# Weight loads move from SyncE's queue to ScalarE's, into ten raw slots and then five

## The chip, the cores and the metric

The kernel runs on one core of one Trainium2 chip. The metric is the time of one execution on the device in microseconds (us), lower is better. Five engines work side by side, each through its own instructions in the order in which they were placed: TensorE (PE, with its weight loads shown as PEld), VectorE (DVE), ScalarE (ACT), GpSimd (POOL) and SyncE (SP), which in this kernel issues every transfer (DMA). The transfers themselves run on 16 DMA engines.

## The reference

Causal attention with a decay, then a gated two-layer block, over 8 batches x 8 heads x 576 tokens x 64 (4608 tokens of 512 features, 2048 hidden):

```python
scores = scale * np.matmul(q, k.transpose(0, 1, 3, 2))
cum = np.cumsum(np.log(np.clip(f, 0.0001, 1.0)), axis=-1)
decay = cum[:, :, :, None] - cum[:, :, None, :]
scores = np.where(causal, -1000000000.0, scores + decay)
attn = np.exp(scores - np.max(scores, axis=-1, keepdims=True))
attn = attn / (np.sum(attn, axis=-1, keepdims=True) + 1e-09)
x = np.matmul(attn, v).transpose(0, 2, 1, 3).reshape(B * S, H * D)
h = x @ w_in
g = h * np.clip(h + 3.0, 0.0, 6.0) / 6.0
out = g @ w_out
```

`w_in` (512 x 2048) and `w_out` (2048 x 512) come as 64-bit floats, 8 MB each; everything else is 32-bit.

## The kernel before

The attention is walked over a list `VH` of stages. Batch 0 is cut in two so that the second layer block can start early: four stages "A" (two heads each, the first 256 queries) and eight stages "B" (one head each, the other 320 queries). Batches 1 to 7 are 56 stages "F" (one head each). For a stage of batch 0 the work is: `load_x` and `load_c` bring q, k and the decay rows; `parts` and `rests` split q and k in two (the low halves are copied between partitions by transfers `T<-TQ`, `T<-TK`); `natural` makes the scores once for the row maximum (PE tile `pn`, DVE `junk`, L490); `max_rows` turns the maxima (`mr`) and sends them by a small transfer `TQ<-mr` into the operand of the real scores; `scores` makes these on PE (`ps`, L548 to L551) and ACT takes the exponential (`pf`, L567; `pf_0` is that of the first stage); `av` multiplies with v (L702), and `x_move` transposes the result into `xT`. The decay rows for all stages come from `decay`: ACT takes a logarithm (`lf`, L169), DVE scans it (`cs`, L172 to L174), and four small transfers `TK<-cs` (L427) bring it to the first two stages.

The weights are brought in 16 chunks of `w_in` and 16 of `w_out`, each 128 x 1024 32-bit words (0.524 MB: 512 values of 64 bits on each of 128 partitions). `w_load` issues a chunk's transfer into a raw slot; `w_decode` makes a 32-bit float of it (ACT Prelu L250, two DVE instructions L251 and L252, which still read the slot) and then takes the sum of squares (ACT Square L256, which writes its junk into the slot, so a slot is free once its Square is done). After four chunks of `w_in` the scale of that group is found (`pow2_scale`), and each chunk is split into two 16-bit halves (`w_split`: ACT L283, and either PE `low` L286, L287 with ACT L288, or DVE L294). `w_out` has one scale for all 16 chunks, so its splits start only when its last chunk is decoded.

Raw slots: three tiles `ring`, which the F stages use for other things later, and for `w_in` three more in the later home of `w2`. Chunk k goes to slot k mod 6 (`w_in`) or k mod 3 (`w_out`). For `w_in` four or five chunks are asked for ahead (`W_AHEAD`). The first eight loads are `pinned`: they stand behind the latest small transfer of the attention in SP's queue.

The generators `w_in_work` and `w_out_work` are advanced by `w_step`, eight times in an A stage, five times in a B stage; `fill` advances the work of the second block (`h_unit`, L781 to L796; `out_unit`, L803 to L815). What is written this way is only a priority: a scheduler places every engine's instructions by a timeline that it works out itself, and gives them the semaphores. For the transfers of both queues it has eight completion counters, DMAHW0 to DMAHW7, which they take in turn; a transfer that takes a counter again waits until the one that had it before has landed.

Of the kernel before, what the change touches and what calls it, by code (L numbers as in the profile page):

```python
# [13 lines left out]
I32 = mybir.dt.int32  # L14
# [6 lines left out]
def kernel(  # L21
# [10 lines left out]
    nc = tc.nc  # L32
# [50 lines left out]
    W_RATE = (8, 5, 4)  # L83
    H_COST = 1.05
    F_RATE = (0.6, 0.45, 1.02)
    PIN = 0
    PIN0 = 1
    LOW_W = 0
    W_GAP = 5
# [11 lines left out]
    NSP = 3  # L101
    PL_POOL = ((3, ), ())
    NAT = ((1, 4, 0), (2, 3))
    B0_POOL = ((0, 0), (1, 1))
    W_AHEAD = (4, 5)
    W_ORDER = 0
    POOL_REST = ((0, 0, 0, 0), (0, 0, 0, 0))
    PIN_V = 1
# [22 lines left out]
    vst = cpool.tile([P, NCH, VR], F32, name="vst")  # L131
# [4 lines left out]
    xT = [cpool.tile([P, NCC, 2, TT // P, 2, 64], F16, name=f"xT{i}") for i in range(3)]  # L136
# [69 lines left out]
    def pinned():  # L206
        return tc.issue_after(small[-1]) if small else nullcontext()


    wide = w_in.dtype == mybir.dt.int64  # L210
    NW = 16
    CW = NCC * DFF // NW
    wsum = cpool.tile([P, 2 * NW], F32, name="wsum")
    ring = [cpool.tile([P, 2 * CW], I32, name=f"ring{i}") for i in range(NRING)]
    gTf = gT.bitcast(F32).rearrange("p a c t -> p (a c t)")
    w2f = w2.bitcast(F32).rearrange("p k a e -> p (k a e)")
    spare = w2.bitcast(I32).rearrange("p k a e -> p (k a e)")
    slots_out = [t[:, :] for t in ring]
    slots_in = slots_out + [spare[:, (2 * h + 9) * CW:(2 * h + 11) * CW] for h in range(NSP)]

    def w_chunk(i, k):

        if i == 0:
            j, c = divmod(k, NCC)
            cols = slice(j * CW, (j + 1) * CW)
            o = (2 * j + c % 2 + NW // 2 * (c // 2)) * CW
            return w_in[c * P:(c + 1) * P, cols], gTf[:, o:o + CW], [t[:, c, cols] for t in w1]
        return (
            w_out[k * P:(k + 1) * P, :], w2f[:, (k + 1) * CW:(k + 2) * CW],
            [w2[:, k, h, :] for h in range(2)],  # L230
        )

    def w_load(i, k, slots):
        src, x, _ = w_chunk(i, k)
        with pinned() if PIN or i == 0 and k < 8 else nullcontext():
            if wide:
                nc.sync.dma_start(slots[k % len(slots)], src.bitcast(I32))
            else:
                nc.sync.dma_start(x, src)

    def w_decode(i, k, slots):

        slot = slots[k % len(slots)]
        f32 = w_chunk(i, k)[1]
        if wide:
            i32 = f32.bitcast(I32)
            hf = slot.bitcast(F32).rearrange("p (n t) -> p n t", t=2)[:, :, 1]
            lo = slot.rearrange("p (n t) -> p n t", t=2)[:, :, 0]

            nc.scalar.activation(f32, hf, AF.Prelu, scale=2.0 ** -112, alpha=2.0 ** 32)  # L250
            nc.vector.tensor_scalar(i32, i32, 3, None, op0=ALU.logical_shift_left)  # L251
            nc.vector.scalar_tensor_tensor(  # L252
                i32, lo, 29, i32, op0=ALU.logical_shift_right, op1=ALU.bitwise_or
            )
        if i == 1 or not GRAM[k // NCC]:
            nc.scalar.activation(  # L256
                slot.bitcast(F32)[:, :CW], f32, AF.Square,
                accum_out=wsum[:, NW * i + k:NW * i + k + 1],
            )

    def w_gram(ks):

        pg = ps_m.tile([P, TT], F32, tag="mm", name=f"gram_{ks[0]}")[:, 0:P]
        n = len(ks) * CW // P
        for c in range(n):
            x = w_chunk(0, ks[c * P // CW])[1].bitcast(BF16)
            x = x.rearrange("p (n t) -> p n t", t=2)[:, c * P % CW:c * P % CW + P, 1]
            nc.tensor.matmul(pg, x, x, start=(c == 0), stop=(c == n - 1))
        junk = p2.tile([P, S], BF16, tag="junk", name=f"jg_{ks[0]}", bufs=1)
        nc.vector.tensor_tensor_reduce(  # L270
            junk[:, 0:P], pg, identf, 1.0, 0.0, ALU.mult, ALU.add,
            accum_out=wsum[:, ks[0]:ks[0] + 1],
        )
        return wsum[:, ks[0]:ks[0] + 1]
# [19 lines left out]
            nc.vector.scalar_tensor_tensor(lo, x, sc, hi, op0=ALU.mult, op1=ALU.subtract)  # L294

    def w_in_work():
        first, ahead = W_AHEAD
        for k in range(first):
            w_load(0, k, slots_in)
        yield  # L300
        for k in range(first, ahead):
            w_load(0, k, slots_in)
        for j in range(NG):
            ks = range(j * NCC, (j + 1) * NCC)
            for k in ks:
                if k + ahead < NW:
                    w_load(0, k + ahead, slots_in)
                w_decode(0, k, slots_in)
                yield
            pm = w_gram(ks) if GRAM[j] else w_sum(ks[0], ks[-1] + 1)  # L310
            yield
            yield from pow2_scale(pm, S1 + j, I1 + j, f"w0{j}")
            eye = None
            if PE_LOW[j]:
                eye = p2.tile([P, DM], F32, tag="o", name=f"eye{j}")[:, 0:P]
                nc.vector.tensor_scalar(
                    eye, identf, scol(S1 + j), -1.0, op0=ALU.mult, op1=ALU.mult
                )
            for k in ks:
                w_split(0, k, scol(S1 + j), eye)  # L320
                yield
            w_in_done.append(j)
# [591 lines left out]
    for i, (kind, n) in enumerate(VH):  # L914
        b, h = divmod(n, H)
# [4 lines left out]
        ahead = i + 2 < NV  # L920
# [99 lines left out]
```

## Time and profile before

| what | us |
|---|---|
| three runs without the profiler | 1083.75, 1084.57, 1087.27 |
| median | 1084.57 |
| the profiled execution | 1083.28 |
| its span, first to last instruction | 1081.5 |
| around the span | 1.8 |
| PE busy in it | 1010.1 |
| DVE, ACT, POOL busy in it | 719.7, 610.1, 413.1 |

The page of the profile gives the busy time of each engine and the span cut in 40 equal slices (27 us each). In the first slices lies what this change touches: the transfers of the weights, their decoding, stages A and B. A matmul's busy time is longer than the time after which the next one starts, so a PE that is shown busy throughout may still have room. An entry such as "idle before <-DMA ring" says what ended the idle time ahead of an instruction.

### The profile page before, as it was taken

How to read it: one execution, taken by the hardware profiler on the slowest of the kernel's cores; microseconds unless marked ns; L12 is line 12 of the kernel's file. 1: busy time of each engine (PE TensorE's matmuls, PEld its weight loads, DVE VectorE, ACT ScalarE, POOL GpSimd, SP SyncE). 2: the span in 40 equal slices, each digit the busy share in tenths (PEclk: the TensorE clock that was granted, in tenths of full speed). 3: DMA queues.
4: the chain of work that ended last, by engine and by line, in shares of the span. 5: the costliest groups of instructions: out<-in, count | busy, mean ns of one | idle time of the engine just before them, and what ended most of it. 6: DMA issues, size and time to landing. Idle time of an engine off the chain costs nothing.

```text
span 1081.5 us, 20281 instructions
## 1 busy us (share of the span) xinstructions
PE 1010.1 (93%) x7074; PEld 577.4 (53%) x7074; DVE 719.7 (67%) x1887; ACT 610.1 (56%) x1285; POOL 413.1 (38%) x505
## 2 busy tenths in 40 slices
PE   2799977988999999999999989999999999999998
PEld 2567854755555555555555545555555555444443
DVE  7869899876885688468865795689668841510520
ACT  4778656845764577356754674477447841621520
POOL 7344455335434445444544444454445420000000
PEclk9989989999999999999999999999999999999999
DMA  8866547767756666667576856675666651000001
GB/s 258 277 172 194 150 105 134 179 127 150 156 114 141 140 146 118 137 129 164 108 139 138 164 113 130 146 166 114 128 140 128 106 112 46 1 10 30 1 1 39
DMA packets 261650, 133.74 MB, mean 124 GB/s; under 512 B 229444, under 2 KB 231036, under 8 KB 261548
## 3 DMA queue, kind: packets, MB, share of 16 engines
q1 hardware_dynamic: 261548, 132.45, 54.7%
q8 instruction: 56, 0.92, 0.3%
q14 instruction: 46, 0.38, 0.1%
HBM read 47.93 MB, written 9.73 MB: 53 GB/s over the span
## 4 chain that ended last, share of the span: by engine, by line
PE 64%; DVE 12%; DMA 9%; issue 5%; ACT 5%; SPq 2%; POOL 2%; DVEq 0%; POOLq 0%; ACTq 0%
PE po L803 10%; PE po L804 10%; PE po L805 10%; PE ph L781 7%; PE ph L782 7%; PE ph L783 7%; DMA vst<-in_vS_dram 3%; PE pn L611 3%; PE pn L608 2%; DVE pp L619 2%; DVE ring L648 2%; DMA T<-TK 1%; DVE gT L796 1%; DMA w<-in_w_in_dram 1%; DVE r L794 1%
## 5 line engine op out<-in xcount | busy, mean ns | idle before, releaser
L781 PE MATMUL ph<-xT,w 128*128 128x512 f16 (+1 forms) x640 | 231.2, 363 | 14.5 <-DVE r L794 9.1
L782 PE MATMUL ph<-xT,w 128*128 128x512 f16 (+1 forms) x640 | 230.2, 363 | 0.0
L783 PE MATMUL ph<-xT,w 128*128 128x512 f16 (+1 forms) x640 | 230.0, 363 | 0.0
L631 ACT ACTIVATE pp<-pp,nb 128x192 f32<-128x192 f32 x280 | 138.5, 552 | 148.8 <-DVE nb L625 145.8
L804 PE MATMUL po<-w,gT 128*128 128x512 f16 x576 | 216.3, 381 | 6.1 <-DVE w L294 6.1
L805 PE MATMUL po<-w,gT 128*128 128x512 f16 x576 | 215.9, 381 | 0.0
L803 PE MATMUL po<-w,gT 128*128 128x512 f16 x576 | 213.6, 381 | 1.1 <-ACT o L814 0.8
L648 DVE TENSOR_TENSOR ring<-pp,ring 128x128 f16<-128x128 f32 (+2 forms) x216 | 131.5, 622 | 84.1 <-ACT ring L645 83.2
L791 ACT ACTIVATE r<-ph,bias_r,SC 128x256 f32<-128x256 f32 (+7 forms) x272 | 144.4, 570 | 28.6 <-PE ph L783 27.9
L794 DVE SCALAR_TENSOR_TENSOR r<-r,ph 128x512 f32<-128x512 f32 (+1 forms) x160 | 100.1, 627 | 88.9 <-ACT r L791 88.6
L458 POOL TENSOR_TENSOR T<-ST,T 64x576 fp32r<-64x576 f32 (+1 forms) x68 | 101.2, 1488 | 143.2 <-DMA T<-TK 133.4
L619 DVE CUSTOM_DVE_ANT_0 pp<-pn,W 128x192 f32<-128x192 f32 x280 | 122.9, 482 | 20.6 <-PE pn L611 16.6
L796 DVE TENSOR_TENSOR gT<-r,gT 128x512 f16<-128x512 f32 (+1 forms) x160 | 118.3, 743 | 27.4 <-ACT gT L795 26.6
L795 ACT CAST gT<-r 128x512 f16<-128x512 f32 (+1 forms) x160 | 91.8, 575 | 75.9 <-DVE r L794 75.8
L608 PE MATMUL pn<-TK,TQ 68*128 68x192 f32 x336 | 124.1, 383 | 5.8 <-issue 5.0
L611 PE MATMUL pn<-T,T 128*128 128x192 f32 x336 | 113.5, 368 | 4.3 <-POOL T L458 4.3
L645 ACT CAST ring<-pp 128x192 f16<-128x192 f32 x280 | 112.9, 452 | 0.0
L455 POOL TENSOR_TENSOR T<-ST,TQ 64x576 fp32r<-64x576 f32 (+2 forms) x68 | 97.6, 1435 | 24.8 <-PE pn L611 18.2
L654 POOL TENSOR_TENSOR ring<-pp,ring 128x128 f16<-128x128 f32 x96 | 61.5, 641 | 105.5 <-ACT ring L645 83.7
L782 PEld LDWEIGHTS <-w 128*128 128x128 f16 x640 | 62.7, 99 | 65.8 <-issue 20.9
L805 PEld LDWEIGHTS <-gT 128*128 128x128 f16 x576 | 56.8, 99 | 74.9 <-issue 13.7
L781 PEld LDWEIGHTS <-w 128*128 128x128 f16 x640 | 63.1, 99 | 62.2 <-issue 14.3
(136 smaller groups left out, 1703.4 us busy)
## 6 DMA issues: line engine op xcount, KB each, us to landing
ST<-in_qk_dram SPq DMA_DIRECT2D x64, 288.0 KB
T<-TK SPq DMA_DIRECT2D x64, 144.0 KB
out_dram<-o SPq DMA_DIRECT2D x36, 256.0 KB
ring<-in_w_out_dram SPq DMA_DIRECT2D x16, 512.0 KB
T<-TQ SPq DMA_DIRECT2D x56, 144.0 KB
vst<-in_vS_dram SPq DMA_DIRECT2D x7, 1040.0 KB
ring<-in_w_in_dram SPq DMA_DIRECT2D x9, 512.0 KB
w<-in_w_in_dram SPq DMA_DIRECT2D x7, 512.0 KB
```

Of the source, the lines that this page charges most:

```text
L608: nc.tensor.matmul(dst, TQ[i][0:D + 4, qs], TK[i][0:D + 4, a:e], start=True, stop=False)
L611: nc.tensor.matmul(dst, T7[j][:, qs], T1[j][:, a:e], start=False, stop=True)
L619: nc.vector.tensor_tensor_reduce(pp[:r, w:w + kw], pn[:r, o:o + kw], W[:r, 4 * P + r - kw:4 * P + r], 1.0, -3.0e38, ALU.add, ALU.max, accu ...
L631: nc.scalar.activation(x_, x_, AF.Exp, bias=nb[:r, e0 + x:e0 + x + 1], scale=0.125)
L648: eng.tensor_tensor(hl[:r, a:a + c * P], pp[:r, at[c] + 64:at[c] + kw], hl[:r, h0[c] + 64:h0[c] + kw], op=ALU.subtract,)
L781: nc.tensor.matmul(ph, w1[0][:, cc, fs_], xh, start=(cc == 0), stop=False)
L782: nc.tensor.matmul(ph, w1[0][:, cc, fs_], xl, start=False, stop=False)
L783: nc.tensor.matmul(ph, w1[1][:, cc, fs_], xh, start=False, stop=(cc == NCC - 1))
L791: nc.scalar.activation(r[:, a:e], ph[:, a:e], AF.Relu, bias=bias_r, scale=scol(A1 + NG * b + fc * NG // NFC))
L803: nc.tensor.matmul(po, gT[:, 0, fc, ts_], w2[:, fc, 0, :], start=(fc == 0), stop=False)
L804: nc.tensor.matmul(po, gT[:, 0, fc, ts_], w2[:, fc, 1, :], start=False, stop=False)
L805: nc.tensor.matmul(po, gT[:, 1, fc, ts_], w2[:, fc, 0, :], start=False, stop=(fc == NFC - 1))
```

## The change

All 32 loads of weights are issued from ACT's queue instead of SP's. `w_in` gets ten raw slots: the three `ring` tiles, two in `vst` (where v of batch 1 and later will stand), two in `xT[1]` (a tile of transposed attention output, first written in stage B), and the three in `w2`. All ten loads are asked for at once, and each further load directly behind the decoding that frees its slot. `w_out` gets five: the `ring` tiles and the two in `vst`. The pinning and its constants are gone.

```diff
-    slots_out = [t[:, :] for t in ring]
-    slots_in = slots_out + [spare[:, (2 * h + 9) * CW:(2 * h + 11) * CW] for h in range(NSP)]
+    vsp = vst.bitcast(I32).rearrange("p c e -> p (c e)")
+    xsp = xT[1].bitcast(I32).rearrange("p a h c l t -> p (a h c l t)")
+    slots_out = [t[:, :] for t in ring] + [vsp[:, 2 * h * CW:2 * (h + 1) * CW] for h in range(2)]
+    slots_in = slots_out + [xsp[:, 2 * h * CW:2 * (h + 1) * CW] for h in range(2)]
+    slots_in += [spare[:, (2 * h + 9) * CW:(2 * h + 11) * CW] for h in range(NSP)]
...
     def w_load(i, k, slots):
         src, x, _ = w_chunk(i, k)
-        with pinned() if PIN or i == 0 and k < 8 else nullcontext():
-            if wide:
-                nc.sync.dma_start(slots[k % len(slots)], src.bitcast(I32))
-            else:
-                nc.sync.dma_start(x, src)
+        if wide:
+            nc.scalar.dma_start(slots[k % len(slots)], src.bitcast(I32))
+        else:
+            nc.scalar.dma_start(x, src)
...
     def w_in_work():
-        first, ahead = W_AHEAD
-        for k in range(first):
+        ahead = len(slots_in)
+        for k in range(ahead):
             w_load(0, k, slots_in)
         yield
-        for k in range(first, ahead):
-            w_load(0, k, slots_in)
         for j in range(NG):
             ks = range(j * NCC, (j + 1) * NCC)
             for k in ks:
+                w_decode(0, k, slots_in)
                 if k + ahead < NW:
                     w_load(0, k + ahead, slots_in)
-                w_decode(0, k, slots_in)
                 yield
```

Line numbers of the changed kernel differ by one or two (the load is L237 before and L238 after; `pf` is L567 and L566). What the scheduler makes of it shows at three places.

**The start of ACT.** Before, ACT's first rows lead straight to the logarithm `lf`, and its first Prelu reads the first chunk:

```order
L161 ACT_TABLE_LOAD
L161 ACTIVATE warm<-warm 1x1 [waits DVE_49]
L169 ACTIVATE lf<-fs 64x576 [waits DVE_49]
L170 ACT_TABLE_LOAD
L170 ACTIVATE warm<-lf 1x1 [waits Activation_49]
L250 ACTIVATE gT<-ring_123 128x512 [waits DMAHW2_49]
```

In the changed kernel (`ring`, `vst`, `xT`, `w` are the slots):

```order
L238 DMA ring_123<-in_w_in_dram 128x1024
L159 ACT_TABLE_LOAD
L159 ACTIVATE warm<-warm 1x1 [waits DVE_49]
L238 DMA ring_124<-in_w_in_dram 128x1024
L238 DMA ring_125<-in_w_in_dram 128x1024
L238 DMA vst<-in_w_in_dram 128x1024
L238 DMA vst<-in_w_in_dram 128x1024 [waits DMAHW0_49]
L238 DMA xT_118<-in_w_in_dram 128x1024 [waits DMAHW1_49]
L238 DMA xT_118<-in_w_in_dram 128x1024 [waits DMAHW2_49]
L238 DMA w_115<-in_w_in_dram 128x1024 [waits DMAHW3_49]
L238 DMA w_115<-in_w_in_dram 128x1024 [waits DMAHW4_49]
L238 DMA w_115<-in_w_in_dram 128x1024 [waits DMAHW5_49]
```

The logarithm comes right behind these rows: ten issues now stand ahead of it, and the last six each wait for a counter, that is for an earlier transfer to land (DMAHW0 was taken by the first chunk, DMAHW3 by the second, DMAHW5 by the third, the others by the loads of f and q, k).

**SP's queue, from the decay rows to the first row maxima.** Before (TK_96 is the operand of the first stage, TK_97 of the second):

```order
L427 DMA TK_96<-cs 2x1x256 [waits DMAHW1_49]
L427 DMA TK_97<-cs 2x1x256 [waits DMAHW2_49,Pool_49]
L427 DMA TK_97<-cs 2x1x256 [waits DMAHW3_49]
L453 DMA T_101<-TQ_93 64x512 [waits DMAHW4_49,Pool_49]
L454 DMA T_99<-TK_96 64x512 [waits DMAHW5_49]
L869 DMA decay_dram<-cs 64x1152 [waits DMAHW6_49]
L237 DMA ring_125<-in_w_in_dram 128x1024 [waits DMAHW7_49,Activation_49]
L237 DMA w_115<-in_w_in_dram 128x1024 [waits DMAHW0_49,Activation_49]
L454 DMA T_100<-TK_97 64x512 [waits DMAHW1_49,Pool_49]
L421 DMA TK_98<-decay_dram 2x2x256 [waits DMAHW6_49,DMAHW2_49]
L453 DMA T_102<-TQ_94 64x512 [waits DMAHW3_49,Pool_49]
L502 DMA TQ_93<-mr_186 1x4x128 [waits DMAHW4_49,DVE_49]
```

In the changed kernel:

```order
L426 DMA TK_96<-cs 2x1x256 [waits DMAHW1_49,DVE_49]
L426 DMA TK_96<-cs 2x1x256 [waits DMAHW3_49]
L426 DMA TK_97<-cs 2x1x256 [waits DMAHW4_49]
L426 DMA TK_97<-cs 2x1x256 [waits DMAHW6_49]
L868 DMA decay_dram<-cs 64x1152 [waits DMAHW0_49]
L452 DMA T_102<-TQ_94 64x512 [waits DMAHW2_49,Pool_49]
L405 DMA ST_103<-in_qk_dram 128x2x256 [waits DMAHW5_49,Pool_49]
L410 DMA ST_104<-in_qk_dram 128x576 [waits DMAHW6_49,Pool_49]
L420 DMA TK_98<-decay_dram 2x2x256 [waits DMAHW0_49]
L501 DMA TQ_93<-mr_192 1x4x128 [waits DMAHW1_49,DVE_49]
```

The weights are gone from SP's queue, but their counters are not: of the four small transfers the first waits for the counter of the 6th chunk (DMAHW1), the second for that of the 8th (DMAHW3), the third for that of the 9th (DMAHW4); `TQ_93<-mr` waits for DMAHW1 again, which the 14th chunk had in between.

**ACT around the first B stage's exponential (`pf_4`).** Before (`w2 <- ring` are Prelus of `w_out`, of which the one into `ring0` is the third):

```order
L250 ACTIVATE w2_115<-ring2_125 128x512
L256 ACTIVATE w2_115,wsum_122<-gT_116 128x512
L567 ACTIVATE pf_3_505<-ps_3_0_506,bias_p_84 128x768
L256 ACTIVATE ring1_124,wsum_122<-gT_116 128x512
L250 ACTIVATE w2_115<-ring0_123 128x512
L734 CAST xhl_2_587<-xf_2_586 128x2x128
L288 ACTIVATE w11_114<-low_5_447 128x512
L288 ACTIVATE w11_114<-low_4_442 128x512
L256 ACTIVATE ring2_125,wsum_122<-w2_115 128x512
L567 ACTIVATE pf_4_600<-ps_4_0_601,bias_p_84 128x640
```

In the changed kernel (the DMA row is the load of the last chunk, the 32nd, and the Prelu from `ring0` decodes it):

```order
L251 ACTIVATE w2_115<-vst_112 128x512
L733 CAST xhl_1_493<-xf_1_492 128x2x128
L238 DMA ring0_123<-in_w_out_dram 128x1024
L257 ACTIVATE vst_112,wsum_122<-w2_115 128x512
L289 ACTIVATE w11_114<-low_5_450 128x512
L257 ACTIVATE vst_112,wsum_122<-w2_115 128x512
L289 ACTIVATE w11_114<-low_4_445 128x512
L251 ACTIVATE w2_115<-ring0_123 128x512
L566 ACTIVATE pf_4_600<-ps_4_0_601,bias_p_84 128x640
```

Ahead of `pf_4` stand now the Prelus of all 32 chunks; before, it was those of 19. The group splits (L283, four times four) and the `low` halves keep their places among the exponentials. DVE's rows follow the same pattern: its first `junk` (the row maximum of the first stage) stood behind the decoding of 4 chunks and stands now behind that of 10; and its first of the 16 splits of `w_out` (L294, after: L295) comes 12 rows earlier and the last 11 rows earlier, the B and F stages being otherwise in nearly the same order.

More of the change, by code (lines that the diff above doesn't have):

```diff
@@ L85 @@
     F_RATE = (0.6, 0.45, 1.02)
-    PIN = 0
     PIN0 = 1
@@ L104 @@
     B0_POOL = ((0, 0), (1, 1))
-    W_AHEAD = (4, 5)
     W_ORDER = 0
```

## The prediction

> **What bounds the kernel now.** I read the page first, then the busy time by stretches, then the start in order of time, then the chain of waits. About 0.3% (3.3 us) is what a measurement of this kernel can tell from no change.
>
> ```profile
> span 1081.5 us, 20281 instructions
> ...
> PE   2799977988999999999999989999999999999998
> ...
> GB/s 258 277 172 194 150 105 134 179 127 150 156 114 141 140 146 118 137 129 164 108 139 138 164 113 130 146 166 114 128 140 128 106 112 46 1 10 30 1 1 39
> ```
>
> PE is shown busy nearly everywhere but in the first slices, and those are where the transfers are dense. The start by stretches (stage A and the first weights, to 66 us; the rest of stages A and B, to 138; the start of F, to 200):
>
> ```profile
> core 0: us, PE busy (x) PEld busy (x) DVE busy (x) ACT busy (x) POOL busy (x), PEclk, DMA share, GB/s
> 0.00:20.00 20.00, 2.53 (x9) 1.87 (x9) 13.32 (x38) 9.27 (x18) 17.98 (x34) 1.00 0.79 238
> 20.00:40.00 20.00, 15.94 (x62) 12.56 (x63) 16.95 (x51) 12.29 (x26) 8.14 (x9) 1.00 0.98 321
> 40.00:66.00 26.00, 17.84 (x86) 12.76 (x85) 18.27 (x62) 18.54 (x40) 9.16 (x9) 0.74 0.69 194
> 66.00:138.00 72.00, 70.35 (x533) 57.43 (x532) 61.45 (x174) 52.49 (x110) 32.35 (x34) 1.00 0.58 172
> 138.00:200.00 62.00, 47.86 (x429) 31.48 (x428) 60.59 (x160) 42.34 (x92) 33.17 (x34) 0.94 0.67 139
> ...
> 0.00:66.00 66.00, 36.32 (x155) 27.19 (x156) 48.54 (x149) 40.10 (x82) 35.29 (x51) 0.90 0.81 246
> ```
>
> So PE idles 29.7 us before 66, 1.65 us from there to 138, and 14.1 us from 138 to 200, where DVE is busy 60.59 of 62. Transfers are full only from 20 to 40 (share 0.98, 321 GB/s), and not from 40 to 66 (194 GB/s): there is room for the weights to come earlier, and that is what the change uses. The question is what stands behind them. The start in order of time:
>
> ```profile
> 2.02 1.41 SPq L237 DMA_DIRECT2D ring<-in_w_in_dram  x3
> ...
> 4.32 0.68 ACT L169 ACTIVATE lf<-fs 64x576 f32<-64x576 f32 x1 [2.08 <-DVE fs L167]
> ...
> 6.87 0.66 ACT L250 ACTIVATE gT<-ring 128x512 f32<-128x512 f32 x1 [0.36 <-DMA ring<-in_w_in_dram]
> ...
> 8.19 0.73 DVE L174 SCALAR_TENSOR_TENSOR cs<-cum,cs 64x576 fp32r<-64x576 f32 x1
> ...
> 8.23 0.67 ACT L250 ACTIVATE gT<-ring 128x512 f32<-128x512 f32 x1 [0.69 <-DMA ring<-in_w_in_dram]
> ...
> 9.00 2.68 SPq L427 DMA_DIRECT2D TK<-cs  x4
> ...
> 12.79 1.20 PE L484 MATMUL pn<-TK,TQ 66*128 66x128 f32 x4 [12.79 <-DMA TK<-cs]
> ...
> 18.35 0.69 SPq L502 DMA_DIRECT2D TQ<-mr  x1
> ...
> 22.20 0.58 PE L548 MATMUL ps<-TQ,TK 97*128 97x256 f32 x1 [4.30 <-DMA TQ<-mr]
> ...
> 24.96 0.90 ACT L567 ACTIVATE pf<-ps,bias_p 128x768 f32<-128x768 f32 x1
> ```
>
> The next exponentials of ACT:
>
> ```profile
> 37.41 0.89 ACT L567 ACTIVATE pf<-ps,bias_p 128x768 f32<-128x768 f32 x1
> ...
> 47.78 0.89 ACT L567 ACTIVATE pf<-ps,bias_p 128x768 f32<-128x768 f32 x1
> ...
> 59.12 0.90 ACT L567 ACTIVATE pf<-ps,bias_p 128x768 f32<-128x768 f32 x1 [1.33 <-PE ps L551]
> ...
> 65.19 0.79 ACT L567 ACTIVATE pf<-ps,bias_p 128x640 f32<-128x640 f32 x1
> ```
>
> The five exponentials are `pf_0` to `pf_4`: stage A is over and the first B stage begins at 65.19. That is the milestone I follow. From there PE has work nearly all the time, so what delays `pf_4` delays the end, less what B then gets back.
>
> **The change part by part.** How many chunks were asked for by 66 us:
>
> ```profile
> L237 SPq DMA_DIRECT2D ring<-in_w_in_dram x9: 327/432/534, 2.0 to 44.8; - x9
> L237 SPq DMA_DIRECT2D w<-in_w_in_dram x7: 328/430/742, 3.5 to 44.2; - x7
> L237 SPq DMA_DIRECT2D ring<-in_w_out_dram x4: 328/428/534, 32.8 to 60.9; - x4
> ```
>
> That is 20 of 32. The sizes of a chunk, of q and k for an A stage, and of a copy between partitions in it:
>
> ```profile
> ring<-in_w_in_dram SPq DMA_DIRECT2D x9, 512.0 KB
> ...
> ST<-in_qk_dram SPq DMA_DIRECT2D x4, 256.0 KB
> ...
> T<-TK SPq DMA_DIRECT2D x4, 128.0 KB
> ```
>
> At 0.524 MB each the 20 chunks are 10.5 MB of the 246 x 66 = 16.2 MB moved; the other 5.7 MB are q, k, v and the copies between partitions.
>
> *The logarithm, +4 us.* `lf` (4.32) now stands behind ten issues, the last of which waits for the third chunk to land. Before, three chunks issued from 2.02 on were read from 6.87 and 8.23 on, and the third would follow 1.4 us later by that spacing. Issued from 0.75 to about 3.5, the third lands at about 8: `lf` at 8.3, +4. Bounds: 0, if the chunks land at once, and +6.
>
> *The decay rows, +9.* `TK<-cs` was issued from 9.00 and PE began at 12.79. Now its second and third transfer wait for the 8th and 9th chunk. Nine chunks are 4.7 MB, f (64 x 576 words), three loads of q and k and three copies 1.3 MB; at 321 GB/s from about 2 us on that is 2 + 6.0/0.321 = 20.7, and with some 2 us to land PE begins at about 22: +9. This takes in the +4 of `lf`.
>
> *The row maxima, +13.* `TQ<-mr` (18.35, scores at 22.20) waits for the 14th chunk: 7.3 MB and 2.2 MB of others (one more copy, two more loads of q and k and the decay rows on top of the 1.3), 2 + 9.5/0.321 = 31.6 for the issue and, with the 3.85 us from issue to scores of before, 35.5. DVE's first `junk` stands behind ten decodings on top.
>
> *The end of stage A, `pf_4`, +11.* ACT and DVE take their rows in order, so `pf_4` cannot come before the 32nd chunk has landed: 16.8 + 5.6 MB of others = 22.4 MB, and 2 + 22.4/0.321 = 72 us if the transfers never pause. They will: ACT issues the loads of `w_out` only as its Squares free five slots, and stands between them at `pf_0` to `pf_3`, which wait for PE, which waits for SP's small transfers, which wait for counters held by chunks. I take 4 us for that, the shortfall that the counters and five slots make when the last chunks are asked for one by one (a chunk's own 0.524/0.321 = 1.6 us and the latency of some 2 us, exposed once): `pf_4` at 76, +11. Lower end: 72, +7. Upper end: the transfers run at the 246 GB/s that the whole start had before, 22.4/0.246 = 91, +26. I stay near the first, since more loads are open at a time than before. ACT itself isn't what holds it:
>
> ```profile
> 36.29 1.22 ACT L250 ACTIVATE gT<-ring 128x512 f32<-128x512 f32 x2
> ...
> 41.49 0.61 ACT L256 ACTIVATE ring<-gT 128x512 f32<-128x512 f32 x1
> 42.01 0.18 ACT L256 ACTIVATION_READ_ACCUMULATOR ring<-gT 128x1 f32 x1
> ```
>
> A chunk costs ACT 0.61 + 0.61 us from start to start (the read lies in it but for 0.1). The 13 chunks that have come ahead of `pf_4` are 16 us on top of the 40.10 that it was busy to 66, thus 56 of 76. The issues come on top of that: SP took 0.43 us for one (the middle value above), 32 are 14 us. ACT's sequencer can issue while the engine still works through rows queued ahead of it, so I count about a third, 5 us, inside the 4 us of pauses and the slack; all of them would make 70 of 76, still no bound.
>
> *Stage B, -5 us.* Behind `pf_4` the decoding of 13 chunks is gone, 16 us of ACT and, by the two rows here, 13 x 1.3 = 17 us of DVE; after them, three pieces of the chain of waits (start, us, what):
>
> ```profile
> L252 DVE SCALAR_TENSOR_TENSOR w<-ring,w 128x512 int32<-128x512 int32 x16 | 12.8, 801 | 0.2
> ...
> L251 DVE TENSOR_SCALAR w<-w 128x512 int32<-128x512 int32 x16 | 8.3, 519 | 3.9 <-ACT w L250 3.9
> ```
>
>
> ```profile
> 48.07 8.26 DMA TQ<-mr
> ...
> 77.89 5.30 DMA ring<-in_w_out_dram
> ...
> 90.48 3.96 DMA ring<-in_w_out_dram
> ```
>
> The two waits for chunks of `w_out`, 9.3 us of chain, go. But PE was idle only 1.65 us from 66 to 138, so what they cost is between 1.65 and 9.3: PE did other rows meanwhile, some of them less densely than it can. I take the middle, 5, for neither row is nearer. PE's own work is next: it cannot get back more than it lost.
>
> *What the queue of SP gains, in the +11.* `TQ<-mr` at 48.07 took 8.26 us, behind weights in the same queue. The changed SP queue has no weights ahead of it, and 0.43 us of issue time saved for each of 32 loads; but its waits for counters hold it all the same until stage A ends. The Trainium skill (DMA: Bandwidth & Descriptors, Issuing engines are not separate DMA queues) speaks against the change as a whole: transfers started by several engines run on the same 16 DMA engines and interleave, and only the issuing sequencer's time is saved. By that rule the rate has no gain at all and the sum stays as it is, with 321 GB/s as the ceiling; that row is from one queue, and no run shown has two.
>
> *The splits of w_out, -1.*
>
> ```profile
> L294 DVE SCALAR_TENSOR_TENSOR w<-w,SC 128x512 f16<-128x512 f32 x16 | 13.7, 859 | 0.1
> ```
>
> From 138 to 200 DVE is the bound, and 16 splits of 0.86 us lie in it. One or two of them now come ahead of it, in DVE's room of stage B: -0.9 to -1.7. Nothing else of F changes place; from 200 us on the order is the same and I cost it at nothing. What hides a stray exchange of rows there is PE's backlog of second-block work; where that is thin it may cost or give 1 us.
>
> *PE ahead, -1.* When ACT reaches `pf_4` late, PE has the scores of the next B stage done already (two buffers): 0 to -2.
>
> Sum: +11 - 5 - 1 - 1 = +4. The profiled execution took 1083.28; it would take 1087.3. It stands 1.3 below the median of the runs, 1084.57, and so the median after is about 1089 (1084.6 + 4).
>
> **The rivals.**
>
> *Faster.* The small transfers no longer stand behind weights in one queue, so that each takes some 3 us, as the one at 18.35 did, instead of 8.26; the pauses don't come about, `pf_4` is late by no more than 5, and B gets back all 9.3 with the splits on top: +5 - 9.3 - 1.2 = -5.5, 1079. For it speaks the free rate from 40 to 66 (194 of 321 GB/s); against it that 72 us for the 32nd chunk is already the best rate seen, so +5 needs a better one. The Trainium skill has this mechanism in the same page (Queues, rings and completion order): each DMA engine takes turns between queues packet by packet. By that the small transfer passes the weights, and the time is that of this rival. The trace has one queue alone and cannot show it.
>
> *No change.* `pf_4` late by 8 to 9, and B, the splits and PE's lead give back as much: within 1081.3 to 1087.8, about 1085. For it: DVE and ACT lose over a quarter of their load in B.
>
> *Slower by much.* Loads issued in order on ACT hold the exponentials and are held by them; the rate stays at the average of before, `pf_4` comes at 91: +26 - 9.3 - 2 = +15, 1099. It decides from the point where ACT's waits for a counter, and not the DMA engines, set when the next chunk comes: then the DMA share between 20 and 70 us is under 0.75, as it was from 40 to 66.
>
> **How the numbers follow.** The forecast (`pf_4` late by 10 to 16, end at 1088 to 1093) has 0.35, faster 0.25, no change 0.28, much slower 0.12. So faster by over 0.3% is 0.25, within 0.3% 0.28, slower 0.47. The likeliest case's own range is 1088 to 1093. The range that leaves out half of the faster end and half of the slow one is 1079 to 1098.
>
> **What would show it.** In the changed profile: `lf` at about 8; the first `pn` at about 22 behind `TK<-cs`; the first scores at about 35; `pf_4` at 72 to 80 with ACT's last Prelu of `w_out` just ahead; a DMA share near 1 to 70 us; no wait for `w_out` from there to 140; the first F stage some 4 us later than before, and equal distances from there. It would be wrong if `pf_4` came before 70 (then the rate was higher or the counters held less than I think), or if the time from `pf_4` to the first F stage shrank by much more or less than 5 us.

## The result: slower, with the start later than forecast

| | before | after |
|---|---|---|
| median of nine runs, us | 1083.75 | 1096.87 |
| lowest to highest | 1080.98 to 1087.27 | 1090.39 to 1103.44 |
| profiled execution | 1083.28 | 1090.39 |
| its span | 1081.5 | 1088.3 |

The ratio is 1.0116 [1.0086, 1.0147]: slower, inside the range, and more so than the 1089 of the forecast. The profiled execution of after is the shortest of its nine, so the trace shows 7.1 us of the 13.1 between the medians. Three single executions that ran in a slower state (2074.17 and 1093.12 of the kernel before, 1302.07 of e12) are left out of the ratios below. The granted clock doesn't explain the loss: it was 0.983 to 0.990 in the nine runs of after, and 0.982 in the profile of before.

The page of after, the same three lines as of before:

```profile
span 1088.3 us, 20259 instructions
...
PE   0389997899899999999999989999999999999998
...
GB/s 280 305 232 85 61 133 123 158 163 151 131 146 135 142 163 114 134 135 169 113 128 137 155 130 128 139 148 138 125 139 125 105 117 46 1 10 30 1 1 39
```

The weights do come earlier: the first three slices carry 280, 305 and 232 GB/s where they had 258, 277 and 172, and the fourth and fifth have 85 and 61 left of 194 and 150. PE's first two slices read 0 and 3 where they read 2 and 7. By stretches (busy us and number of instructions of PE, PEld, DVE, ACT, POOL, then clock, DMA share, GB/s):

```profile
0.00:20.00 20.00, 0.00 (x0) 0.00 (x0) 7.98 (x20) 5.90 (x10) 16.24 (x33) 1.00 0.92 320
20.00:40.00 20.00, 3.12 (x12) 2.44 (x12) 18.41 (x43) 14.77 (x37) 4.68 (x3) 1.00 0.81 250
40.00:66.00 26.00, 19.05 (x75) 14.26 (x73) 22.01 (x65) 18.79 (x41) 10.24 (x11) 1.00 0.91 285
66.00:138.00 72.00, 68.03 (x483) 54.55 (x483) 50.64 (x160) 45.27 (x90) 27.42 (x31) 0.95 0.42 108
138.00:200.00 62.00, 52.36 (x409) 35.13 (x406) 55.56 (x153) 37.91 (x77) 38.28 (x34) 0.97 0.57 129
0.00:66.00 66.00, 22.17 (x85) 16.71 (x85) 48.40 (x126) 39.46 (x86) 31.16 (x46) 1.00 0.88 285
```

To 66 us PE is busy 22.17 instead of 36.32. From 66 to 138 it looks nearly as busy as before (68.03 against 70.35), but it ends 483 matmuls instead of 533. From 138 to 200 it is the other way round: 52.36 us of PE instead of 47.86, and DVE down from 60.59 to 55.56. The start in order of time:

```profile
6.40 4.24 ACTq L238 DMA_DIRECT2D xT<-in_w_in_dram  x2
...
10.37 0.61 POOL L445 TENSOR_SCALAR TK<-ST 64x512 fp32r<-64x512 f32 x1 [0.20 <-DMA ST<-in_qk_dram]
...
10.68 3.60 ACTq L238 DMA_DIRECT2D w<-in_w_in_dram  x3
...
13.52 0.61 POOL L445 TENSOR_SCALAR TK<-ST 64x512 fp32r<-64x512 f32 x1 [0.95 <-DMA ST<-in_qk_dram]
...
14.33 0.68 ACT L167 ACTIVATE lf<-fs 64x576 f32<-64x576 f32 x1 [11.68 <-DMA xT<-in_w_in_dram]
...
18.13 1.75 DVE L253 SCALAR_TENSOR_TENSOR gT<-ring,gT 128x512 int32<-128x512 int32 x1
19.81 0.74 DVE L172 SCALAR_TENSOR_TENSOR cs<-cum,cs 64x576 fp32r<-64x576 f32 x1
...
20.58 2.62 SPq L426 DMA_DIRECT2D TK<-cs  x4
...
23.91 2.05 PE L483 MATMUL pn<-TK,TQ 66*128 66x128 f32 x8 [23.91 <-DMA TK<-cs]
...
33.66 0.28 DVE L489 CUSTOM_DVE_ANT_0 junk<-pn,W 128x128 bf16<-128x128 f32 x1
...
36.86 0.27 DVE L500 TENSOR_SCALAR mr<-ptm 4x128 fp32r<-4x128 f32 x1
...
37.16 0.69 SPq L501 DMA_DIRECT2D TQ<-mr  x1
...
39.47 0.58 PE L547 MATMUL ps<-TQ,TK 97*128 97x256 f32 x1
```

This list is the way to read such a delay: for each row, which engine held it last. `lf` is held by ACT's own queue, whose tenth issue ends just before it: six issues wait for counters, as the order showed. The two longest of these waits are not for chunks. They end with the seventh issue at 10.31 and the ninth at 13.47, just as POOL gets the first and the second load of q and k (10.37, 13.52); the tenth follows 0.37 us after the ninth. But `TK<-cs` is not held by counters: `cs` ends at 20.55 and the transfer goes at 20.58; between `lf` and `cs` DVE decodes weights too. And `TQ<-mr` is not held either (`mr` ends at 37.13, the transfer goes at 37.16): the scores `pn` are there by 25.96, and `junk` starts 7.7 us later because the decoding of ten chunks stands ahead of it on DVE. The end of stage A, with the first and the last split of `w_in` (L284) and the first matmul of the scores that `pf_4` reads (`ps`):

```profile
26.30 0.61 ACT L257 ACTIVATE vst<-gT 128x512 f32<-128x512 f32 x1
...
48.77 0.15 DVE L279 TENSOR_REDUCE wm<-wsum 128x1 f32<-128x4 f32 x1
...
53.11 0.71 ACT L284 ACTIVATE w<-gT,SC 128x512 f16<-128x512 f32 x1
...
79.26 0.33 ACTq L238 DMA_DIRECT2D ring<-in_w_out_dram  x1
...
80.69 0.50 PE L547 MATMUL ps<-TQ,TK 97*128 97x320 f32 x1
...
83.06 0.66 ACT L251 ACTIVATE w<-ring 128x512 f32<-128x512 f32 x1
83.62 1.41 ACT L566 ACTIVATE pf<-ps,bias_p 128x640 f32<-128x640 f32 x2
...
103.87 2.56 ACT L284 ACTIVATE w<-gT,SC 128x512 f16<-128x512 f32 x4 [0.23 <-DVE SC L190]
```

The scale, the first split, the scores of `pf_4`, the last split and the last Prelu of `w_out` before:

```profile
26.02 0.15 DVE L278 TENSOR_REDUCE wm<-wsum 128x1 f32<-128x4 f32 x1
...
32.67 2.54 ACT L283 ACTIVATE w<-gT,SC 128x512 f16<-128x512 f32 x4
...
63.90 0.31 PE L548 MATMUL ps<-TQ,TK 97*128 97x320 f32 x1
...
89.52 2.55 ACT L283 ACTIVATE w<-gT,SC 128x512 f16<-128x512 f32 x4
...
115.72 0.66 ACT L250 ACTIVATE w<-ring 128x512 f32<-128x512 f32 x1 [0.88 <-DMA ring<-in_w_out_dram]
```

So the last chunk of `w_out` is decoded at 83.06 instead of 115.72, and yet the first layer's weights are ready 14 us later (the last group's split at 103.87 instead of 89.52), and the splits of `w_out`, for which its early chunks were meant, begin on ACT at 149.5 instead of 136.8. The fourth Square, with which the first group's sums are complete, starts at 26.30, but the scale (`wm`) stands on DVE behind rows of the attention that are late, and comes at 48.77, where it came at 26.02 before. The second block of work, whose matmuls fill PE's gaps in the B stages, starts on PE at 102.79 instead of 85.90. It begins with the columns of the first group, which were being split from 53.11 on, and ahead of the last split; but it needs the output of all four A stages; the last transfers of that (`xT<-xhl`) are issued from 91.85 on instead of 72.35. So it goes with the late attention, not with the late splits:

```profile
102.79 0.28 PE L780 MATMUL ph<-xT,w 128*128 128x256 f16 x1
...
0.00:120.00 120.00, 72.20 (x413) 55.71 (x414) 87.99 (x251) 75.69 (x158) 52.30 (x70) 0.97 0.70 212
```

and before:

```profile
85.90 0.27 PE L781 MATMUL ph<-xT,w 128*128 128x256 f16 x1
...
0.00:120.00 120.00, 89.28 (x545) 69.59 (x545) 94.61 (x275) 82.36 (x172) 58.64 (x77) 0.94 0.73 221
```

By 120 us PE is 132 matmuls behind. F gives part of it back: from 200 to 400 us PE ends 1533 matmuls instead of 1473.

### The profile page after: what moved, and what is told of

Same layout as the page of the kernel before. It is cut to its first block, busy times and chain, and to the rows that moved or that the text cites. A ratio compares the mean times of both kernels' runs of the same rounds, so it can differ in the third digit from the quotient of the medians.

```text
span 1088.3 us, 20259 instructions
## 1 busy us (share of the span) xinstructions
PE 1007.7 (93%) x7074; PEld 576.0 (53%) x7074; DVE 717.2 (66%) x1887; ACT 610.8 (56%) x1285; POOL 417.8 (38%) x505
## 4 chain that ended last, share of the span: by engine, by line
PE 64%; DVE 14%; DMA 8%; issue 5%; ACT 5%; SPq 2%; POOL 1%; ACTq 0%; DVEq 0%; POOLq 0%
PE po L802 10%; PE po L803 10%; PE po L804 10%; PE ph L780 7%; PE ph L781 7%; PE ph L782 7%; DMA vst<-in_vS_dram 3%; PE pn L610 2%; PE pn L607 2%; DVE pp L618 2%; DVE ring L647 2%; PE pav L701 2%; ACT pp L630 1%; DVE r L793 1%; SPq L754 1%
## 5 line engine op out<-in xcount | busy, mean ns | idle before, releaser
L795 DVE TENSOR_TENSOR gT<-r,gT 128x512 f16<-128x512 f32 (+1 forms) x160 | 114.8, 720 | 30.8 <-ACT gT L794 30.0
L454 POOL TENSOR_TENSOR T<-ST,TQ 64x576 fp32r<-64x576 f32 (+2 forms) x68 | 101.1, 1487 | 21.4 <-PE pn L610 15.7
L781 PEld LDWEIGHTS <-w 128*128 128x128 f16 x640 | 62.4, 98 | 63.5 <-issue 18.3
L782 PEld LDWEIGHTS <-w 128*128 128x128 f16 x640 | 62.2, 98 | 62.8 <-issue 8.2
L780 PEld LDWEIGHTS <-w 128*128 128x128 f16 x640 | 62.9, 98 | 61.4 <-issue 13.1
```

Of the source, the lines that this page charges most:

```text
L780: nc.tensor.matmul(ph, w1[0][:, cc, fs_], xh, start=(cc == 0), stop=False)
L781: nc.tensor.matmul(ph, w1[0][:, cc, fs_], xl, start=False, stop=False)
L782: nc.tensor.matmul(ph, w1[1][:, cc, fs_], xh, start=False, stop=(cc == NCC - 1))
```

## The experiments

Ratios are against runs of before on the same chip, with a 95% interval. "First h" is the first matmul of the second block. "End of B" is the start of stage B's last exponential. All rows are from one profile each; before has `pf_0` 24.96, `pf_4` 65.19, first h 85.90, 545 matmuls by 120 us and the end of B at 133.10, after 46.64, 83.62, 102.79, 413 and 148.90.

| run | median us | ratio | `pf_0` | `pf_4` | first h | matmuls by 120 | end of B |
|---|---|---|---|---|---|---|---|
| e1 after, again | 1093.2 | 1.0109 [1.0074, 1.0144] | 45.54 | 83.06 | 102.83 | 413 | 148.48 |
| e2 slots of before, ACT, no pins | 1103.29 | 1.0173 [1.0143, 1.0204] | 36.07 | 73.1 | 103.44 | 398 | 150.34 |
| e12 e2, loads held behind `pf_0` | 1082.78 | 1.001 [0.9984, 1.0036] | 24.45 | 64.18 | 88.51 | 522 | 135.35 |
| e5 after's slots, SP, no pins | 1103.63 | 1.0173 [1.0144, 1.0202] | 38.89 | 77.63 | 96.78 | 448 | 145.84 |
| e8 before, 32 tiny issues on ACT | 1084.7 | 1.002 [0.9994, 1.0046] | 24.31 | 60.29 | 81.27 | 559 | 130.88 |
| e7 the `w_in` half alone | 1098.16 | 1.0112 [1.0082, 1.0141] | 46.49 | 79.15 | 103.46 | 376 | 152.43 |
| e4 the `w_out` half alone | 1095.73 | 1.0121 [1.0099, 1.0143] | 24.89 | 69.69 | 88.94 | 479 | 144.67 |
| e6 five slots of `w_out`, SP | 1087.25 | 1.0032 [1.0013, 1.0051] | 25.76 | 63.56 | 84.29 | 528 | 138.65 |
| e3 after, three loads first | 1098.15 | 1.0145 [1.012, 1.0169] | 43.22 | 83.47 | 101.24 | 394 | 152.54 |
| e9 after, `junk` first | 1096.57 | 1.0136 [1.0106, 1.0166] | 38.80 | 79.42 | 102.41 | 404 | 149.26 |
| e10 after, attention first | 1101.06 | 1.019 [1.0157, 1.0223] | 31.94 | 69.63 | 98.91 | 393 | 151.41 |
| e11 before, first h held | 1097.18 | 1.0155 [1.0118, 1.0191] | 25.28 | 65.04 | 104.19 | 471 | 130.16 |

**e1: after, unchanged.** For its size, and for a second trace.

> The changed kernel once more, unaltered, for a second profiled execution and for its scatter (nine runs lay between 1090.39 and 1103.44, those of before between 1080.98 and 1087.27). Theory A (the loss arises at the start, from rows that stand in order behind the chunks on ACT and DVE, and from counters): median 1092 to 1100, the logarithm at 12 to 16 us, the first scores at 36 to 44, pf_4 at 80 to 90, and the time from pf_4 to the end within 4 us of the first profile's 1004.7; if this execution is longer than 1090, the start accounts for the difference. Rival (the scatter is not of the start): the same milestones within 1 us of the first profile and the whole difference behind 200 us.

Its span is 1089.7, `pf_4` comes at 83.06 and the first h at 102.83: the second trace repeats the first.

**Who issues, or what is held back: e2, e5, e8, e12.** e2 takes the kernel before and moves the issue alone; with it the pins go, as in the change:

```diff
-        with pinned() if PIN or i == 0 and k < 8 else nullcontext():
-            if wide:
-                nc.sync.dma_start(slots[k % len(slots)], src.bitcast(I32))
+        if wide:
+            nc.scalar.dma_start(slots[k % len(slots)], src.bitcast(I32))
```

> The slots, the order of loads and the look-ahead of before (six slots and five loads ahead for the first layer, three for the second), but every load issued by ACT: the change of queue alone. Theory A: the logarithm stands behind four issues only and DVE's first row maximum behind five decodings, so the start is near that of before: first scores at 21 to 28, pf_4 at 64 to 72, median 1081 to 1088. Rival Q (the second queue itself costs: ACT's in-order issues, the shared counters, interleaved transfers): median 1091 or more, with most of the +13 of the change.

e5 takes the changed kernel and issues its loads from SP, in the same code order, without pins:

```diff
-            nc.scalar.dma_start(slots[k % len(slots)], src.bitcast(I32))
+            nc.sync.dma_start(slots[k % len(slots)], src.bitcast(I32))
```

> The changed kernel with its ten and five slots, but all loads issued by SP (not pinned): only the queue is undone. After the first four runs two theories stand. Theory W (what is put ahead: weights, their decoding and the counters that they hold come ahead of the attention's first steps, whoever issues them): median 1091 to 1102, pf_4 at 78 to 90. Theory Q (issues from ACT cost by themselves: they stand in order among ACT's rows, and their counters among SP's): median 1086 or less, pf_4 at 70 or less.

Both are 1.7% slower than before, by their medians more than after itself, though the intervals still touch. Six slots or ten, ACT or SP: without the pins the attention's start is late in each (`pf_0` at 36.07 and 38.89). e8 gives ACT of the kernel before 32 issues of four bytes each, one behind each Square:

```diff
+            nc.scalar.dma_start(dump[:, NW * i + k:NW * i + k + 1], wsum[0:1, NW * i + k:NW * i + k + 1])
```

> The kernel before, and beside it 32 transfers of 4 bytes issued by ACT, each behind the Square of a chunk: the place of an issue in ACT's order, its time and its completion counter, without moving a weight. Theory Q: 1088 or more. Theory W: 1085 or less, within 3 us of the kernel before.

1.002 [0.9994, 1.0046]: no cost that can be told from none, and at most 0.46%. e12 is e2 with one thing put back: every load after the first four is placed on ACT behind `pf_0`, the first exponential.

```diff
-            nc.scalar.dma_start(slots[k % len(slots)], src.bitcast(I32))
+            with tc.issue_after(pfs[0]) if pfs else nullcontext():
+                nc.scalar.dma_start(slots[k % len(slots)], src.bitcast(I32))
```

> e2 (slots and order of loads of before, all loads by ACT, 1103 median) with one thing added: ACT issues the first four loads at once and every further one only behind the first exponential pf_0, as the pins of before held the loads behind the attention's small transfers. Theory B (the loss of e2 came from loads that went ahead of the attention's first transfers, which the pins had kept back): pf_0 at 24 to 28 (36.1 in e2), first h at 86 to 95 (103.4), median 1083 to 1092. Theory Q (ACT's issues in order cost by themselves): median 1096 or more.

```profile
19.10 0.68 SPq L503 DMA_DIRECT2D TQ<-mr  x1
...
20.84 0.58 PE L549 MATMUL ps<-TQ,TK 97*128 97x256 f32 x1 [0.31 <-DMA TQ<-mr]
...
24.45 0.90 ACT L568 ACTIVATE pf<-ps,bias_p 128x768 f32<-128x768 f32 x1 [6.35 <-PE ps L552]
24.46 0.33 ACTq L238 DMA_DIRECT2D w<-in_w_in_dram  x1
```

The queue of ACT carries all 32 chunks and shares its counters with SP's, and the kernel runs as before (1.001). In e2 the same steps stand at:

```profile
25.97 0.68 SPq L501 DMA_DIRECT2D TQ<-mr  x1
...
36.07 0.88 ACT L566 ACTIVATE pf<-ps,bias_p 128x768 f32<-128x768 f32 x1
```

The two kernels differ in that hold alone, and by 1.6%. So the issuing engine and the shared counters cost nothing that shows once the loads are held back; what costs in e2 is that the weights, and the decoding that follows them on ACT and DVE, are let in ahead of the attention's first steps; the hold puts off both together and doesn't part them. (The hold of e12 is not the pins themselves: those bound the first eight loads, each to the latest small transfer.)

**Which half: e7, e4, e6.** e7 leaves `w_out` as before (three slots, SP, unpinned) and gives `w_in` its ten slots from ACT:

```diff
-    slots_out = [t[:, :] for t in ring] + [vsp[:, 2 * h * CW:2 * (h + 1) * CW] for h in range(2)]
+    slots_out = [t[:, :] for t in ring]
...
-            nc.scalar.dma_start(slots[k % len(slots)], src.bitcast(I32))
+            (nc.sync if i else nc.scalar).dma_start(slots[k % len(slots)], src.bitcast(I32))
```

> The first half of the change alone: the first layer's weights by ACT into ten slots, the second layer's by SP into three slots as before. Theory W and Q: the start as in the changed kernel (logarithm at 14, first scores at 36 to 42), and the median at 1090 to 1098. Rival H (the whole loss comes from the second layer's loads in five slots, as e4 alone had it): 1087 or less in spite of the late start.

The whole loss is there with `w_in` alone (1.0112). e4 and e6 leave `w_in` as before and give `w_out` five slots, two of them in `vst`; e4 loads them from ACT, each behind the second exponential (`pf_1`), e6 from SP, behind the second `TQ<-mr`:

```diff
+            with tc.issue_after(pfs[1]):
+                w_load(1, k, slots_out)
...
-                nc.sync.dma_start(slots[k % len(slots)], src.bitcast(I32))
+                (nc.scalar if i else nc.sync).dma_start(slots[k % len(slots)], src.bitcast(I32))
```

> The kernel before, with the first layer's weights as they were (SP, six slots), and only the second layer's loads issued by ACT, into five slots, each behind the second exponential in ACT's order. It tells the second half of the change apart. Theory A: the start is that of before (pf_4 at 63 to 68), the waits for chunks of w_out in stage B (9.3 us of the chain of before) go in part: median 1077 to 1084. Rival Q (loads from ACT cost by themselves): 1087 or more.

> The kernel before with five slots for the second layer's weights as in e4, but its loads issued by SP, each behind the second transfer of row maxima: against e4 (1095.7 median, +12) only the queue differs. Theory W: 1090 to 1098, since the same loads come as early. Theory Q: 1086 or less.

e6 costs 0.3%, e4 1.2%, with first h at 84.29 and 88.94. Why the same slots cost some 9 us more from ACT, with another point of release, is not settled: the two edits differ in both, and no run parts them (the expectation of e6, that only the queue differs, overlooked the second). The halves don't add up either (1.0112 and 1.0121 against 1.0116 together).

**The order at the start: e3, e9, e10.** Each puts a late step of the attention back in its place. e3 issues three loads before `lf` and the other seven behind it:

```diff
-        for k in range(ahead):
+        for k in range(3):
             w_load(0, k, slots_in)
         yield
+        for k in range(3, ahead):
+            w_load(0, k, slots_in)
```

> The changed kernel, but only three loads are asked for at first and the other seven behind the logarithm on ACT. Theory A: the logarithm comes at 4.5 to 7 (14.3 in the changed kernel), PE begins at 15 to 20 (23.9), but ACT's first exponential still stands behind the Prelus of 16 chunks and DVE's first row maximum behind 8 decodings, so that pf_0 is at 35 to 43 (46.6) and pf_4 at 74 to 81 (83.6): median 3 to 7 us under that of the unaltered changed kernel. Rival C (only the counters count, since the small transfers wait for chunks anyhow): PE begins at 21 or later, and the median is within 2 us of the changed kernel's. Rival L (the logarithm is the whole loss): the whole +13 goes, 1086 or less.

```profile
7.13 0.68 ACT L167 ACTIVATE lf<-fs 64x576 f32<-64x576 f32 x1 [4.48 <-DVE fs L165]
...
15.78 1.29 PE L485 MATMUL pn<-TK,TQ 66*128 66x128 f32 x4 [15.78 <-DMA TK<-cs]
...
43.22 0.88 ACT L568 ACTIVATE pf<-ps,bias_p 128x768 f32<-128x768 f32 x1
```

`lf` is 7.2 us earlier than in after and `pn` 8.1, but `pf_0` only 3.4, and the time doesn't move (1.0145). e9 puts DVE's decoding from the fifth chunk on behind the first stage's `junk`:

```diff
-            nc.vector.tensor_scalar(i32, i32, 3, None, op0=ALU.logical_shift_left)
+            with tc.issue_after(seen[3]) if i == 0 and k >= 4 else nullcontext():
+                nc.vector.tensor_scalar(i32, i32, 3, None, op0=ALU.logical_shift_left)
...
+            seen.append(jd.ins)
```

> The changed kernel with one order fixed: DVE decodes the chunks from the fifth on only behind the four row maxima of the first stage (in the changed kernel nine chunks were decoded ahead of the first). What the runs so far leave is theory W, the weights' rows ahead of the attention, and in it two causes. Theory D (the decoding rows in DVE's and ACT's order hold the attention): the first row maximum at 25 to 28 (33.7), first scores at 29 to 34 (39.5), pf_0 at 33 to 40 (46.6), median 3 to 7 us under the changed kernel's 1094 to 1097. Theory T (the transfers and the counters that hold them are the limit, and DVE's order is only paced by them): first scores at 36 or later, or pf_4 unchanged at 80 to 86, median within 2 us of the changed kernel's.

```profile
26.16 0.28 DVE L491 CUSTOM_DVE_ANT_0 junk<-pn,W 128x128 bf16<-128x128 f32 x1
...
34.38 0.58 PE L550 MATMUL ps<-TQ,TK 97*128 97x256 f32 x1 [6.35 <-DMA TQ<-mr]
```

`junk` is 7.5 us earlier, the scores 5.1, the time unchanged (1.0136). e10 does e3's part and holds both halves of the decoding behind the attention, stage by stage: the Prelus from the 8th, 14th, 17th and 19th chunk on behind `pf_0` to `pf_3`, DVE's rows from the 5th, 8th and 14th behind the `junk` of the first three stages:

```diff
+    PF_AT = (7, 13, 16, 18)
+    JK_AT = (4, 7, 13)
...
+            n = NW * i + k
+            a = [e for e, m in enumerate(PF_AT) if n >= m]
+            with tc.issue_after(pfs[a[-1]]) if a else nullcontext():
...
+            a = [e for e, m in enumerate(JK_AT) if n >= m]
+            with tc.issue_after(seen[4 * a[-1] + 3]) if a else nullcontext():
```

> The changed kernel's loads, slots and queue, but the attention goes first in the orders of ACT and DVE: three loads ahead of the logarithm, DVE's decodings from the fifth, eighth and fourteenth chunk on behind the row maxima of the first, second and third stage, ACT's Prelus from the 8th, 14th, 17th and 19th chunk on behind the exponentials pf_0 to pf_3, about where they stood before. Theory D: the start comes near that of before, pf_0 at 27 to 34, pf_4 at 66 to 75, and at least half of the loss goes: median 1090 or less. Theory T: pf_4 at 78 or later, median 1093 or more.

```profile
69.63 1.44 ACT L579 ACTIVATE pf<-ps,bias_p 128x640 f32<-128x640 f32 x2
...
93.65 0.33 ACTq L240 DMA_DIRECT2D ring<-in_w_out_dram  x1
97.63 0.66 ACT L259 ACTIVATE w<-vst 128x512 f32<-128x512 f32 x1 [1.32 <-DMA vst<-in_w_out_dram]
...
103.27 2.55 ACT L294 ACTIVATE w<-gT,SC 128x512 f16<-128x512 f32 x4
```

Stage A now ends 14.0 us earlier than in after, 4.4 later than before, and the ratio is the highest of all (1.019), though not clear of those of e2 and e5. ACT's order is stuck once more behind `w_out`, now in the B stages; the fourth group is split at 103.27, as in after. The output of stage A leaves late all the same (its last `xT<-xhl` go from 92.86 on, 72.35 before), and stage B ends at 151.41. So `pf_4`, the milestone of the forecast, is not what sets the time.

**The start of the second block: e11.** The kernel before, with the weights as they were; the first h matmul is held on PE behind the scores of the fifth B stage, and its units are queued from there:

```diff
+        held = tc.issue_after(last_ps[LATE - 1]) if t == 0 and c0 == 0 else nullcontext()
...
-                units.append(one(0, 0, QA))
+                late.append(LATE)
...
+        if i in late:
+            units.append(one(0, 0, QA))
```

> The kernel before, its loads untouched, but the second block's first rows on PE (the h matmuls of the first 256 tokens, from 85.9 us on) are held behind the scores of the fifth B stage, some two stages later. In the ten kernels run so far the PE time lost by 120 us goes with the start of h (81 us: 48 lost, 86: 50, 89: 58, 97: 61, 99: 67, 103: 65 to 69), not with pf_4. Theory S (the start of h sets the loss: until then PE has nothing to fill the gaps of the B stages with): h at 96 to 106, the loss by 120 us up by 8 to 15, median 1090 to 1097. Rival F (h's lateness goes with the loss but doesn't make it: the same work fills later gaps): median within 3 us of the kernel before.

```profile
65.04 0.79 ACT L570 ACTIVATE pf<-ps,bias_p 128x640 f32<-128x640 f32 x1
...
104.19 0.61 PE L786 MATMUL ph<-xT,w 128*128 128x256 f16 x2
...
0.00:120.00 120.00, 89.99 (x471) 69.82 (x471) 89.83 (x263) 75.89 (x155) 58.11 (x76) 0.86 0.72 220
```

Stage A ends on time (65.04), first h is 18 us late, and the kernel loses 1.55%. Holding the second block alone can thus cost as much as the change: PE is shown busy (89.99 of 120), but with 471 matmuls in place of 545. It is not the way in which after loses. In e11 stage B ends even earlier than before (130.16 against 133.10, after 148.90), and by 120 us only matmuls of the second block are missing (60 for 144); after has 74 of these and lacks 62 of others on top. And the granted clock is lower in e11: of the 74 matmuls that are missing in all by 120 us, 62 are missing from 90 to 110, where the clock was 0.50 and 0.59 in the two halves and 1.00 in both before. Over the whole span it was 0.965 (before 0.982, after 0.989). An estimate from that: the 1010 us of PE of before would be 18 us longer at such a clock, and the span grew by 14.5. Whether the hold costs by gaps that stay unfilled or by the clock, and whether the clock is low because of the hold, no run here shows.

## Why the prediction was right and where it was wrong

The direction was right and its ground too: the attention waits at the start while the weights come first. Step by step:

- *The logarithm*: +10.0, not +4. The mechanism was right (ACT stands at issues that wait for counters); the size wasn't, nor the counter. Not the third chunk's came free last but those of two loads of q and k, at about 10.3 and 13.5, since four chunks and the loads of f, q and k were under way together, at 320 GB/s over the first 20 us. The load of f itself was late by some 3 us for the same reason, which the working had left out: e3, where `lf` waits for f alone, has it at 7.13.
- *The decay rows*: +11.1 for +9 (23.91 against "about 22"), with the wrong cause. The counters of the 8th and 9th chunk were not what came last; `lf` (+10.0) was, and the decoding on DVE ahead of `cs` (from `lf` to the end of `cs` 6.2 us instead of 4.6).
- *The row maxima*: first scores at 39.47, +17.3 for +13. Here "`junk` stands behind ten decodings on top" was the cause, and the 14th chunk's counter none: the transfer left 0.03 us after its data were there, and took 2.3 us to the scores where I had put 3.85.
- *`pf_4`*: +18.4 for +11, with the wrong bound. It does stand behind the Prelu of the 32nd chunk (83.06, then 83.62), which was asked for at 79.26 only. But the scores that it reads are made on PE from 80.69 on, 63.90 before, so 16.8 of the 18.4 are there already, without that chunk. The transfers weren't the bound either: 108 GB/s from 66 to 138.
- *Stage B gives back 5, F 2 with PE's lead*: the last exponential of B came 15.8 us late, so B gave back 2.6. The first exponential of F is 13.9 late (156.4 against 142.5), the last one 6.8 (896.0 against 889.2), and so is the end: F itself gave back 7, where the working had costed everything from 200 us on at nothing. By what means is not shown. It wasn't the splits of `w_out`: by place in the order they stand earlier, but the 16 on DVE run from 151.6 to 203.6, 139.3 to 191.4 before. That DVE fell from 60.59 to 55.56 in the stretch to 200 is no sign of them, since B lasts until about 150 there.
- *The sum*: +4 forecast, +7.1 in the profiled execution, +13.1 between the medians. That the profiled sum came near is in part luck: `pf_4` was 7 us later than forecast, and F gave back 7 more. The 6 us that the short execution doesn't have are not in its trace, and stay open.

The step that failed is "That is the milestone I follow. From there PE has work nearly all the time, so what delays `pf_4` delays the end, less what B then gets back". e10 and e4 show it: `pf_4` only 4.4 and 4.5 us late, 1.9 and 1.2% lost, and B gave nothing back there but ended 18.3 and 11.6 us late. Two later milestones go with the loss. The first h matmul is late in the other kernels that lost over 1% (e1, e2, e3, e5, e7, e9, e10, e11: 96.8 to 104.2) and near its old place in those within 0.4% (e6, e8, e12: 81.3 to 88.5); only e4 (88.94) lost without it. The end of stage B parts all runs but e11: 144.7 to 152.5 in those that lost over 1%, e4 among them, 130.9 to 138.7 in the three others. That is a pattern of one profile for each run, not a cause shown; e11 shows that holding the second block alone can cost as much, by another way. The second thing missed is the removal of the pins, of which the working spoke nowhere, though the diff shows it: e12 against e2 shows that holding the loads back is worth the whole loss of e2. For the ten slots this is argued, not shown.

The rival "faster" had its short transfer (2.3 us), but that was asked for 18.8 us later than before. The rival "slower by much" named a DMA share under 0.75 from 20 to 70 us; it was 0.81 and 0.91 to 66, and the loss came all the same, after a start that the order on DVE and ACT had made late.

Not tried: the ten slots with their loads held behind `pf_0`. No kernel here beat the one before.

## What to carry to other kernels

Data that arrive early help only if the rows that use them stand early on their engines; here the first group was decoded at 27 us and scaled at 49, behind attention rows that the early decoding had itself made late. Before moving an issue, look for what held it back (a pin, a place behind another row), and keep that in the move. Follow a milestone well behind the change (here the end of stage B told more than the end of stage A), and count finished matmuls, not busy time.

## What the hardware showed that was not expected

The rate had no ceiling at the 321 GB/s that I took from before. From 40 to 50 us of after, with loads from two queues:

```profile
40.00:50.00 10.00, 5.57 (x27) 5.12 (x26) 8.52 (x17) 7.38 (x17) 2.82 (x3) 1.00 1.00 353
```

and from 20 to 40 of e6, with SP's queue alone:

```profile
20.00:40.00 20.00, 15.17 (x56) 11.87 (x57) 16.84 (x48) 11.99 (x25) 8.81 (x10) 1.00 1.02 339
```

The stretches differ in length and content, so that two queues are faster than one is not shown. A small transfer with weights in the other queue alone took 2.3 us from issue to use in after. One in e4, where weights stood in both queues (SP had issued three chunks from 41.58 to 45.94, ACT two from 46.24 on), took 6.68 us in the chain of waits:

```profile
48.46 6.68 DMA TQ<-mr
```

No run here says on what that depends. A busy PE says little of its pace: 89.99 us for 471 matmuls in e11, at a granted clock of 0.86, 89.28 us for 545 before, at 0.94.
